# Attention values and output projections on two 64-row tiles of the matmul array, in two passes with the halves exchanged

## The chip, the cores and the metric

The kernel runs on one core of one Trainium2 chip. The metric is the time of one execution on the device in microseconds (us); the median of several runs is quoted. The profile's span is about 1.8 us shorter than the time of the same run. The execution of the kernel before that was profiled took 929.19 us, 1.0 above the median of its timed runs.

Engines are named as the profile names them: PE is the matrix engine (TensorE), PEld its weight loads, DVE VectorE, ACT ScalarE, POOL GpSimd.

## The reference

The input is one sequence of 2048 rows and 640 columns. After a layer norm, two branches follow; the change touches only the attention branch.

```python
q = (xn @ wq).reshape(B, Sq, 32, 192)              # 32 heads of 192
k, v = k_cache[:, :, -512:], v_cache[:, :, -512:]  # the last 512 keys
scores = einsum("bhqd,bhkd->bhqk", q, k) * 192 ** -0.5
o = einsum("bhqk,bhkd->bhqd", softmax(scores), v)
s = o.reshape(B, Sq, 32 * 192) @ wo                # 6144 -> 640
g = silu(mlp(xn))                                  # gated MLP, 640 -> 1536 -> 640
return x + s * g
```

## The kernel before

The attention works in units: four heads (a group g) and 512 query rows. There are 32 units. Units are taken two at a time; a pair is called a block here. A block first does all scores of its two units, interleaved with the query products of the next two (the stage S), then all values of its two units, interleaved with the output projections of the two units before (the stage V).

Queries and scores have contractions split into 64 rows, so they run on two row tiles of the array: `r = slice(i * H2, (i + 1) * H2)` with `H2 = 64`. The query product has a contraction of 128 rows, so it is done in two passes. In pass one, tile 0 makes the lower half's share of output 0 and tile 1 the upper half's share of output 1. In pass two they exchange outputs. Between the passes VectorE copies two columns of the result into `seen`, for no other purpose than to make pass two wait until pass one's writes have landed. Values and projections used the whole array:

```python
    def values(u, h, k):                       # one head: 512 rows x 192 (+1: the softmax sum)
        e = E[u, h // 2]
        o4 = wide(k).rearrange("p (q n) -> p q n", q=TQ)
        for q in range(TQ):                    # 4 x 4 matmuls of 128 rows x 193 columns
            for c in range(KC):
                nc.tensor.matmul(o4[:, q, 0:DH + 1], lhsT=e[:, c, h % 2, q * P:(q + 1) * P],
                                 rhs=vbuf[:, h, c, 0:DH + 1], start=(c == 0), stop=(c == KC - 1))
        ...
        nc.vector.reciprocal(rden[:], o4[:, :, DH:DH + 1])
        nc.vector.tensor_tensor(o_st[u][:, :, h * DH:(h + 1) * DH], o4[:, :, 0:DH],
                                rden[:].to_broadcast([P, TQ, DH]), ALU.mult)

    def project(u, q, k, out_eng):             # 128 rows: 6 x (512 + 128) columns
        for cc in range(GC):
            for d0, d1 in ((0, 512), (512, D)):
                nc.tensor.matmul(wide(k)[:, d0:d1], lhsT=oT[u][:, cc, q * P:(q + 1) * P],
                                 rhs=wo[:, cc, d0:d1], start=(cc == 0), stop=(cc == GC - 1))
        ...                                    # g == 0: copy; g > 0: acc = result + acc
                                               # last g: times the gate, plus acc, out

    order = (2, 3, 0, 1)
    for u0 in range(0, NU - 2, 2):             # one block
        for u in (u0, u0 + 1):                 # stage S
            for i, what in enumerate(((0, 0), (1, 0), (0, 1), (1, 1), (2, 0), None, (2, 1), None)):
                scores(u, *sc[i], i % 2)
                if what is not None:
                    queries(u + 2, what[0], 2 + (what[0] + u) % 2, what[1])
        ...
        for u in (u0, u0 + 1):                 # stage V
            for q in range(4):
                if u0 > 0:
                    values(u, q, order[2 * q % 4])
                    project(u - 2, q, order[(2 * q + 1) % 4], nc.sync)
                else:
                    values(u, q, order[q])
            turn_out(u)
```

The last argument of each function is the PSUM tile: there are four (0 to 3), each of two banks, and all matmuls of the kernel write to these four. Stage S uses 0 and 1 for scores and 2 and 3 for queries; stage V uses 2, 3, 0, 1 in turn.

The softmax here doesn't subtract the row's maximum and nothing guards it: scores larger than these inputs give would overflow.

## Time and profile before

The time is 928.18 us (927.81 to 928.33, 4 runs).

| what | reading |
|---|---|
| PE busy | 919.2 us of a span of 927.4 |
| PE share of the chain that ended last | 97% |
| granted clock | 0.999 |
| one block (S + V), from first score to first score | 47.23 us |
| PE waiting, in all | 3.2 us, all in start and tail |

The page's table of busy times (engine, us, share of the span, number of instructions), its two lines of the chain, and its four costliest matmul groups (line, operation, output and inputs, shape, count; then busy us and mean ns of one; then idle time before):

```profile
PE 919.2 (99%) x8004; PEld 547.2 (59%) x8004; DVE 467.2 (50%) x736; ACT 302.8 (33%) x333; POOL 126.0 (14%) x152
...
PE 97%; DMA 1%; DVE 1%; SPq 0%; issue 0%; ACT 0%; DVEq 0%; ACTq 0%
PE bank L457 21%; PE bank L421 21%; PE bank L437 18%; PE bank L403 18%; PE bank L250 10%; PE bank L262 6%; PE bank L369 1%; DMA wu_sb<-in_B_w_up_dram 1%; PE bank L300 1%; DVE gate L466 1%; DVE o_sb L461 1%; DMA oT<-o_st 1%; SPq L449 0%; PE bank L230 0%; ACT xnT L236 0%
...
L421 PE MATMUL bank<-xnT,wq_sb 64*128 64x512 bf16 x1800 | 223.7, 376 | 0.0
L457 PE MATMUL bank<-wo_sb,oT 128*128 128x512 bf16 x1344 | 200.8, 299 | 0.0
L403 PE MATMUL bank<-qT,kT 64*128 64x512 bf16 x1536 | 198.4, 376 | 0.0
L437 PE MATMUL bank<-vbuf,E 128*128 128x193 bf16 x2048 | 189.5, 247 | 0.0
```

L421 are the queries, L457 the projections (the mean of 299 ns mixes matmuls of 512 and of 128 columns), L403 the scores, L437 the values. The idle column is 0.0: by this page PE waits for nobody. The mean of one matmul (376 ns for a query) is not what a matmul costs in a stream, because matmuls overlap on record. What counts is the distance from one start to the next. It can be read from the timeline, where neighbours of one kind are merged (start, duration, engine and line, operation, count). Here is PE around a block end of the kernel before, and on DVE the evacuation (the copy out of PSUM) of the last values group; DVE's other instructions are left out:

```profile
257.01 1.50 PE L437 MATMUL bank<-vbuf,E 128*128 128x193 bf16 x16
258.35 1.79 PE L457 MATMUL bank<-wo_sb,oT 128*128 128x512 bf16 x12
258.76 0.96 DVE L443 TENSOR_TENSOR o_st<-bank,rden 128x768 bf16<-128x768 f32 x1
260.07 0.82 PE L403 MATMUL bank<-qT,kT 64*128 64x512 bf16 x6
260.73 1.24 PE L421 MATMUL bank<-xnT,wq_sb 64*128 64x512 bf16 x10
```

From 257.01 to 258.35, 16 values matmuls take 1.34 us: 83.4 ns each by the single records. From 260.73 the ten query matmuls, five pairs, take 1.08 us in the records: 216 ns per pair. From 258.35 to 260.07 a projection takes 1.72 us, but the same step between two values groups takes 1.63; the difference is the mode switch from 128 to 64 rows.

And the table of PE's waits, complete, says where PE stood still (us in total, times, longest):

```profile
PE bank L190 <- DVE eps_t L182: 1.2, 1, 1.2
PE bank L300 <- DMA wg_sb<-in_B_w_gate_dram: 1.0, 1, 1.0
PE bank L457 <- DMA oT<-o_st: 0.6, 1, 0.6
PE bank L300 <- DMA wu_sb<-in_B_w_up_dram: 0.4, 1, 0.4
```

### The profile page before, as it was taken

The page shows a single profiled execution, that of the slowest core. Times are in us where ns is not written, and L with a number is a line of the kernel's source. Part 1 is how long each engine was busy: PE and PEld are TensorE (multiplying, and loading weights), DVE is VectorE, ACT ScalarE, POOL GpSimd, SP SyncE. Part 2 cuts the span into 40 slices and gives each one's busy share as a digit, 9 for nine tenths or more (in the row PEclk, how much of TensorE's full clock was granted, in tenths as well). Part 3 has the DMA queues.
Part 4 walks back from the last instruction along what each step waited for, and adds up shares of the span by engine and source line. Part 5 has one row for each costly group of instructions (what it writes and reads, how often), then busy time and mean ns, then how long its engine had stood idle before and what let it go on. Part 6 is the DMA issues. An engine that isn't in the chain of part 4 may idle for free.

```text
span 927.4 us, 18043 instructions
## 1 busy us (share of the span) xinstructions
PE 919.2 (99%) x8004; PEld 547.2 (59%) x8004; DVE 467.2 (50%) x736; ACT 302.8 (33%) x333; POOL 126.0 (14%) x152
## 2 busy tenths in 40 slices
PE   8999999999999999999999999999999999999997
PEld 6445454465756565656565656566666656565665
DVE  5452522444645464545454555545554545454567
ACT  3222222255141424242423333332324242415240
POOL 1000110001002000200020011001100110175720
PEclk9999999999999999999999999999999999999999
DMA  9310340115424233333424152415251515253625
GB/s 318 80 22 8 88 86 1 43 60 87 82 58 111 78 69 70 97 92 41 97 87 103 39 99 78 111 35 104 65 111 40 110 61 98 66 115 96 102 74 125
DMA packets 162686, 76.68 MB, mean 83 GB/s; under 512 B 140944, under 2 KB 158176, under 8 KB 162608
## 3 DMA queue, kind: packets, MB, share of 16 engines
q1 hardware_dynamic: 155424, 53.64, 27.1%
q0 software_dynamic: 5808, 20.52, 7.9%
q8 instruction: 62, 1.02, 0.5%
q10 hardware_dynamic: 1376, 1.38, 0.4%
q14 instruction: 16, 0.13, 0.1%
HBM read 39.45 MB, written 2.62 MB: 45 GB/s over the span
## 4 chain that ended last, share of the span: by engine, by line
PE 97%; DMA 1%; DVE 1%; SPq 0%; issue 0%; ACT 0%; DVEq 0%; ACTq 0%
PE bank L457 21%; PE bank L421 21%; PE bank L437 18%; PE bank L403 18%; PE bank L250 10%; PE bank L262 6%; PE bank L369 1%; DMA wu_sb<-in_B_w_up_dram 1%; PE bank L300 1%; DVE gate L466 1%; DVE o_sb L461 1%; DMA oT<-o_st 1%; SPq L449 0%; PE bank L230 0%; ACT xnT L236 0%
## 5 line engine op out<-in xcount | busy, mean ns | idle before, releaser
L407 ACT ACTIVATE E<-bank 128x1024 bf16<-128x1024 f32 x256 | 255.8, 1024 | 456.8 <-PE bank L403 456.6
L421 PE MATMUL bank<-xnT,wq_sb 64*128 64x512 bf16 x1800 | 223.7, 376 | 0.0
L457 PE MATMUL bank<-wo_sb,oT 128*128 128x512 bf16 x1344 | 200.8, 299 | 0.0
L403 PE MATMUL bank<-qT,kT 64*128 64x512 bf16 x1536 | 198.4, 376 | 0.0
L437 PE MATMUL bank<-vbuf,E 128*128 128x193 bf16 x2048 | 189.5, 247 | 0.0
L437 PEld LDWEIGHTS <-E 128*128 128x128 bf16 x2048 | 168.6, 98 | 18.0 <-issue 6.4
L428 DVE CAST qT<-bank 128x1024 bf16<-128x1024 f32 x90 | 110.2, 1225 | 128.5 <-PE bank L421 128.5
L457 PEld LDWEIGHTS <-oT 128*128 128x128 bf16 x1536 | 121.0, 98 | 79.0 <-issue 1.3
L421 PEld LDWEIGHTS <-wq_sb 64*128 64x128 bf16 x1800 | 93.1, 100 | 102.2
L403 PEld LDWEIGHTS <-kT 64*128 64x128 bf16 x1536 | 74.0, 94 | 89.8 <-issue 4.8
L443 DVE TENSOR_TENSOR o_st<-bank,rden 128x768 bf16<-128x768 f32 x128 | 122.6, 958 | 4.4
L472 DVE TENSOR_TENSOR acc<-bank,acc 128x640 f32<-128x640 f32 x96 | 79.2, 825 | 43.3 <-PE bank L457 43.2
L118 POOL DMA_DIRECT2D vbuf<-in_A_v_cache_dram x28 | 21.1, 755 | 306.9 <-PE bank L437 304.0
L426 DVE COPY seen<-bank 128x2 f32<-128x2 f32 x90 | 14.4, 160 | 93.8 <-PE bank L421 93.8
L442 DVE RECIPROCAL rden<-bank 128x4 f32<-128x4 f32 x128 | 23.4, 183 | 65.1 <-PE bank L437 65.1
L250 PE MATMUL bank<-xnT,wu_sb 128*128 128x512 bf16 x220 | 54.7, 379 | 0.0
L250 PE MATMUL bank<-xnT,wg_sb 128*128 128x512 bf16 x220 | 54.7, 379 | 0.0
L262 PE MATMUL bank<-wd_sb,hT 128*128 128x512 bf16 (+1 forms) x384 | 52.8, 299 | 0.0
L256 DVE TENSOR_TENSOR hT<-bank,sig 128x512 bf16<-128x512 f32 x44 | 30.3, 690 | 43.7 <-ACT sig L253 43.7
L253 ACT ACTIVATE sig<-bank 128x512 bf16<-128x512 f32 x44 | 26.3, 597 | 68.4 <-PE bank L250 65.2
L262 PEld LDWEIGHTS <-hT 128*128 128x128 bf16 x384 | 29.7, 98 | 23.1
L250 PEld LDWEIGHTS <-wu_sb 128*128 128x128 bf16 x220 | 21.5, 98 | 26.0
(51 smaller groups left out, 317.7 us busy)
## 6 DMA issues: line engine op xcount, KB each, us to landing
wo_sb<-in_A_wo_dram SPq DMA_DIRECT2D x7, 960.0 KB, 5.3
wq_sb<-in_A_wq_dram POOLq DMA_DIRECT2D x7, 960.0 KB, 6.0
k_st<-in_A_k_cache_dram POOLq DMA_DIRECT2D x14, 384.0 KB, 5.2
vbuf<-in_A_v_cache_dram POOLq DMA_DIRECT2D x28, 192.0 KB, 3.3
row<-in_A_x_dram POOLq DMA_DIRECT2D x16, 160.0 KB, 2.8
oT<-o_st SPq DMA_TRANSPOSE x128, 2.6
x_sb<-in_A_x_dram SPq DMA_DIRECT2D x3, 640.0 KB, 9.4
wd_sb<-in_B_w_down_dram SPq DMA_DIRECT2D x1, 1920.0 KB, 12.9
```

Source lines behind the costliest of these rows:

```text
L250: nc.tensor.matmul(bank[k][:, half, 0:r1 - r0], lhsT=w[:, c, f * P:(f + 1) * P], rhs=xnT[:, b, c, r0:r1], start=(c == 0), stop=(c == NCD - 1))
L253: nc.scalar.activation(sig[:, 0:r1 - r0], bank[k][:, 0, 0:r1 - r0], AF.Sigmoid)
L256: nc.vector.tensor_tensor(hT[b][:, f, r0:r1], bank[k][:, 1, 0:r1 - r0], sig[:, 0:r1 - r0], ALU.mult)
L262: nc.tensor.matmul(wide(k)[:, d0:d1], lhsT=hT[b][:, f, q * P:(q + 1) * P], rhs=wd_sb[:, f, d0:d1], start=(f == 0), stop=(f == NF - 1))
L403: nc.tensor.matmul(bank[k][:, i, :], lhsT=kT[r, pr, j, c * P:(c + 1) * P], rhs=q[r, pr * DJ + j, :], start=(j == 0), stop=(j == DJ - 1))
L407: nc.scalar.activation(E[u, pr][:, c, :, :], bank[k][:], AF.Exp, scale=scale_qk)
L421: nc.tensor.matmul(bank[k][:, half, :], lhsT=wq[r, c, col:col + DJ * (P - 1) + 1:DJ], rhs=xnT[r, b, c, :], start=(c == 0 and not second), ...
L428: nc.vector.tensor_copy(qT[u][:, 2 * m:2 * m + 2, :], bank[k][:])
L437: nc.tensor.matmul(o4[:, q, 0:DH + 1], lhsT=e[:, c, h % 2, q * P:(q + 1) * P], rhs=vbuf[:, h, c, 0:DH + 1], start=(c == 0), stop=(c == KC ...
L443: nc.vector.tensor_tensor(o_st[u][:, :, h * DH:(h + 1) * DH], o4[:, :, 0:DH], rden[:].to_broadcast([P, TQ, DH]), ALU.mult)
L457: nc.tensor.matmul(wide(k)[:, d0:d1], lhsT=oT[u][:, cc, q * P:(q + 1) * P], rhs=wo[:, cc, d0:d1], start=(cc == 0), stop=(cc == GC - 1))
L472: nc.vector.tensor_tensor(acc[:, t, :], wide(k)[:, 0:D], acc[:, t, :], ALU.add)
```

## The change

The intent: let the whole attention run on two 64-row tiles, so that PE no longer switches between the modes. Values and projections are split as the queries were: two passes, halves exchanged, a tiny copy between the passes. To fill the time between the passes, two jobs are interleaved: values pass one, projection pass one, values pass two, projection pass two. The last eight projections stay on the full array.

```diff
     def values(u, h, k):
-        for q in range(TQ):
-            for c in range(KC):
-                nc.tensor.matmul(o4[:, q, 0:DH + 1], lhsT=e[:, c, h % 2, q * P:(q + 1) * P],
-                                 rhs=vbuf[:, h, c, 0:DH + 1], start=(c == 0), stop=(c == KC - 1))
+        for turn in range(2):
+            for qq in range(TQ // 2):
+                for c in range(KC):
+                    for i in range(2):
+                        r = slice(i * H2, (i + 1) * H2)
+                        q = (i ^ turn) * (TQ // 2) + qq
+                        nc.tensor.matmul(o4[:, q, 0:DH + 1],
+                                         lhsT=e[r, c, h % 2, q * P:(q + 1) * P],
+                                         rhs=vbuf[r, h, c, 0:DH + 1],
+                                         start=(turn == 0 and qq == 0 and c == 0),
+                                         stop=(turn == 1 and c == KC - 1), skip_group_check=True)
+            if turn == 0:
+                nc.vector.tensor_copy(seen[:, DJ, :], bank[k][:, :, 0])
+                yield
... (reciprocal and o_st as before)
-    def project(u, q, k, out_eng):
+    def project(u, q, k, out_eng, two=True):
+        res = bank[k][:, :, 0:HD]              # two halves of 320 columns, one per bank
+        for turn in range(2 if two else 1):
+            for cc in range(GC):
+                for i in range(2):
+                    r = slice(i * H2, (i + 1) * H2) if two else slice(0, P)
+                    half = i ^ turn
+                    nc.tensor.matmul(res[:, half, :], lhsT=oT[u][r, cc, q * P:(q + 1) * P],
+                                     rhs=wo[r, cc, half * HD:(half + 1) * HD], ...)
+            if two and turn == 0:
+                nc.vector.tensor_copy(seen[:, DJ + 1, :], bank[k][:, :, 0])
+                yield
... (what follows reads res in place of wide(k)[:, 0:D])
+    def together(*jobs):
+        for _ in range(2):
+            for j in jobs:
+                next(j, None)
...
-            for q in range(4):
-                if u0 > 0:
-                    values(u, q, order[2 * q % 4])
-                    project(u - 2, q, order[(2 * q + 1) % 4], nc.sync)
-                else:
-                    values(u, q, order[q])
+            if u0 > 0:
+                for q in range(4):
+                    together(values(u, q, order[2 * q % 4]),
+                             project(u - 2, q, order[(2 * q + 1) % 4], nc.sync))
+            else:
+                for q in (0, 2):
+                    together(values(u, q, order[q]), values(u, q + 1, order[q + 1]))
... (in the tail likewise: projections two at a time, values two at a time;
...  the last eight projections with two=False)
```

More of the change, by code (lines that the diff above doesn't have):

```diff
@@ L393 @@
     oT = {}
-    seen = acc_pool.tile([P, DJ, 2], F32, name="seen")
+    seen = acc_pool.tile([P, DJ + 2, 2], F32, name="seen")
     load_wo(0)
@@ L449, in turn_out @@
             nc.sync.dma_start_transpose(oT[u][:, :, q * P:(q + 1) * P], o_st[u][:, q, :])
-    def project(u, q, k, out_eng):
+    HD = D // 2
+    def project(u, q, k, out_eng, two=True):
         g, b = u // NB, u % NB
@@ L454, in project, with cols @@
         t = b * TQ + q
-        for cc in range(GC):
-            for d0, d1 in ((0, 512), (512, D)):
-                nc.tensor.matmul(wide(k)[:, d0:d1], lhsT=oT[u][:, cc, q * P:(q + 1) * P],
-                                 rhs=wo[:, cc, d0:d1], start=(cc == 0), stop=(cc == GC - 1))
+        def cols(x):
+            return x.rearrange("p (i n) -> p i n", i=2)
+        res = bank[k][:, :, 0:HD]
[5 more added lines that the diff above has]
+                    nc.tensor.matmul(res[:, half, :], lhsT=oT[u][r, cc, q * P:(q + 1) * P],
+                                     rhs=wo[r, cc, half * HD:(half + 1) * HD],
+                                     start=(turn == 0 and cc == 0),
+                                     stop=(cc == GC - 1 and (turn == 1 or not two)),
+                                     skip_group_check=two)
+            if two and turn == 0:
+                nc.vector.tensor_copy(seen[:, DJ + 1, :], bank[k][:, :, 0])
+                yield
         if g == NG - 1:
             o_sb = fin.tile([P, D], F32, name="o_sb", bufs=2)
-            nc.vector.tensor_tensor(o_sb[:], wide(k)[:, 0:D], gate[:, t, :], ALU.mult)
+            nc.vector.tensor_tensor(cols(o_sb[:]), res, cols(gate[:, t, :]), ALU.mult)
             r_sb = gate[:, t, :]
@@ L469, in project @@
         elif g == 0:
-            nc.vector.tensor_copy(acc[:, t, :], wide(k)[:, 0:D])
+            nc.vector.tensor_copy(cols(acc[:, t, :]), res)
         else:
-            nc.vector.tensor_tensor(acc[:, t, :], wide(k)[:, 0:D], acc[:, t, :], ALU.add)
+            nc.vector.tensor_tensor(cols(acc[:, t, :]), res, cols(acc[:, t, :]), ALU.add)
         if g == NG - 2:
@@ L477, in project @@
             nc.gpsimd.tensor_tensor(acc[:, t, :], acc[:, t, :], x_sb[:], ALU.add)
+        yield
+    def together(*jobs):
+        for _ in range(2):
+            for j in jobs:
+                next(j, None)
     sc = [(pr, c) for pr in range(2) for c in range(KC)]
@@ L516 @@
         scores(*sc[i], order[i % 4])
-    for q in range(2):
-        project(u - 2, q, q, nc.sync)
+    together(*(project(u - 2, q, q, nc.sync) for q in range(2)))
     for i in range(6, 12):
         scores(*sc[i], order[(i - 6) % 4])
-    for q in range(2, 4):
-        project(u - 2, q, q - 2, nc.sync)
+    together(*(project(u - 2, q, q - 2, nc.sync) for q in range(2, 4)))
     for i in range(12, 16):
         scores(*sc[i], order[i % 4])
-    for q in range(4):
-        project(u - 1, q, order[q], nc.sync)
+    for q in (0, 2):
+        together(*(project(u - 1, q + i, order[q + i], nc.sync) for i in range(2)))
     for v in (u, u + 1):
-        for h in range(4):
-            values(v, h, order[h])
+        for h in (0, 2):
+            together(*(values(v, h + i, order[h + i]) for i in range(2)))
         turn_out(v)
     for q in range(4):
-        project(u, q, order[q], nc.sync)
+        together(project(u, q, order[q], nc.sync, False))
     for q in range(4):
-        project(u + 1, q, order[q], nc.scalar if q < 3 else None)
+        together(project(u + 1, q, order[q], nc.scalar if q < 3 else None, False))
 _INS = ['A_x', 'A_k_cache', 'A_v_cache', 'A_wq', 'A_wo', 'B_x', 'B_w_gate', 'B_w_up', 'B_w_down']
```

## The prediction

> **What bounds the kernel.** TensorE: PE is busy 919 of 927 us (busy table), the chain of waits is 97% PE, and the granted clock is 1.0. The wait table shows PE waiting for nothing but 3 us of start and tail.
>
> **Issue times from the trace (start to start).** Values: 83.4 ns per full-array 128x193 matmul, 1.335 us per head. Projection: 216 + 56 ns per 512+128 columns, 1.63 us per tile. Queries and scores, already on two 64-row tiles: 216 ns per pair of 512 columns, the two members 3 to 7 ns apart. A pair costs what one full matmul costs, so splitting values and projections saves no streaming: 16 pairs of about 83 ns, and 12 of (320/512 of 213 + 2.7) = 136 ns, again 1.63 us.
>
> **What it saves.** Only mode switches. The Trainium skill ("TensorEngine Tiling (Array Packing)", Key Properties) says changing the tiling mode drains the TensorE; this trace agrees: the step from 64 to 128 rows takes 308 instead of 209 ns, the way back 151 instead of 56, so about 97 ns each. 29 of 31 switches go: -2.8 us.
>
> **What it adds.** 3488 matmuls (hidden, if issue keeps up) and about 250 tiny VectorE copies between the passes (160 ns, as those of the queries). The skill (same page, Gotcha 1) says row tiles may not access one PSUM bank simultaneously; hence pass two waits for that copy. VectorE works in order: the copies come behind the evacuations.
>
> Per values+projection step (2.97 us) VectorE needs 217 (reciprocal) + 875 (o_st) + 742 (acc) + 2x77 ns, about 2.0 us (spacings from the trace). Following order: the values copy ends about 1.38 us after the step's start and pass two wants to start at 1.48. It just fits.
>
> It does not fit in three places:
> 1. Block ends. The last values group now ends 0.82 us before the scores instead of 1.63, so its o_st (bank 0, which the first score needs) ends 0.6 us late: 14 blocks, about +8.5 us.
> 2. Values beside values (first block): the copy sits behind two o_st of 0.96 us, about 0.6 us per pair: +2 us.
> 3. Tail: projections beside projections with two 0.82 us multiplies or adds each, and values pairs: +6 us.
>
> A recurrence over both engines with these durations reproduces the kernel before (47.25 us per block against 47.23 in the trace) and gives about +14 us for the change. 60 ns more release latency or a slower 2x320 evacuation opens the wait in about 100 steps (+5 us). Values now need four PE instructions per 83 ns; the densest stretch of this trace does two per 56 ns. Each 10 ns more per pair would cost about 15 us.
>
> **Prediction:** 943 us, 80% range 935 to 964. Faster by over 2%: 0.01; within 2%: 0.62; slower by over 2%: 0.37.
>
> **What would show it.** Right: values pairs at 83 ns and projection pairs at 136; score matmuls waiting on o_st (0.5 to 0.7 us, once per block); PE waiting on the copies little in the steady steps, 0.6 us or more in first block and tail; the gaps of 308 and 151 ns gone; PE idle rising from 8 to over 20 us. Wrong: no wait at block ends, or values pairs at 95 ns or more.
>
> **What would make it wrong.** Issue rate (slower, over 950); pairs of short matmuls streaming better than full ones (faster); the copy's wait opening in every step.

## The result

The changed kernel takes 942.66 us (942.01 to 943.09, 4 runs) against 928.18 (927.81 to 928.33, 4 runs). The ratio is 1.0156, with a 95% interval of 1.0138 to 1.0174. Here and below, a ratio is the mean time of one kernel's fast runs over that of the other's fast runs of the same rounds, so it is not quite the ratio of the medians quoted.

The lines of the page after that answer to those of before:

```profile
PE 920.3 (98%) x11474; PEld 630.1 (67%) x11492; DVE 486.7 (52%) x984; ACT 302.7 (32%) x333; POOL 125.7 (13%) x152
...
PE 93%; DVE 5%; DMA 1%; issue 1%; DVEq 0%; ACT 0%; ACTq 0%
PE bank L421 21%; PE bank L482 20%; PE bank L403 18%; PE bank L443 17%; PE bank L250 10%; PE bank L262 5%; DVE o_st L456 3%; PE bank L369 1%; DVE o_sb L492 1%; DVE gate L497 1%; PE bank L300 1%; DMA wu_sb<-in_B_w_up_dram 1%; DVE rden L455 0%; PE bank L230 0%; DVE seen L450 0%
...
L482 PE MATMUL bank<-wo_sb,oT 64*128 64x320 bf16 x2688 | 222.8, 296 | 0.0
L443 PE MATMUL bank<-vbuf,E 64*128 64x193 bf16 x4096 | 212.6, 243 | 3.9 <-DVE seen L450 3.9
L403 PE MATMUL bank<-qT,kT 64*128 64x512 bf16 x1536 | 201.3, 376 | 6.7 <-DVE o_st L456 6.5
```

PE has 3,470 more matmuls on record and is busy only 1.1 us longer; that the tiles do not slow it down is shown by the starts below, since busy times rest on modelled ends. What is new is DVE's 5% in the chain, chiefly `o_st` (L456), and two idle figures that were 0.0. The waits of PE after, longest first; what is left out are waits of the start, as before, and two of 1.1 and 0.3 us in the tail:

```profile
PE bank L403 <- DVE o_st L456: 6.5, 14, 0.6
PE bank L443 <- DVE seen L450: 3.9, 7, 1.4
...
```

Fourteen waits of a score for `o_st`: one at the end of each of the 15 blocks but the last. A block now takes 47.82 us instead of 47.23. Timeline of PE and DVE at such a block end (weight loads, other engines and DVE's other instructions left out):

```profile
260.53 0.84 PE L443 MATMUL bank<-vbuf,E 64*128 64x193 bf16 x16
261.20 0.99 PE L482 MATMUL bank<-wo_sb,oT 64*128 64x320 bf16 x12
261.63 0.96 DVE L456 TENSOR_TENSOR o_st<-bank,rden 128x768 bf16<-128x768 f32 x1
262.64 0.82 PE L403 MATMUL bank<-qT,kT 64*128 64x512 bf16 x6 [0.45 <-DVE o_st L456]
```

The 16 half matmuls of a values pass, eight pairs, take 0.67 us from start to start (260.53 to 261.20), which is 83 ns per pair: exactly what a full matmul took before. The last values group ends where the projection's pass two begins, 0.82 us before the scores could start (261.20 + 12/2 x 0.136 = 262.01). Its evacuation `o_st` ends at 262.59 (261.63 + 0.96), so the first score, which writes the same PSUM tile 0, starts at 262.64 instead of 262.01: 0.63 us lost. Before, the whole projection of 1.63 us stood between the two, and the evacuation ended at 259.72, 0.35 us before the first score (260.07).

Note that the table says 0.45 us where 0.63 were lost. The profile counts idle time from the *end* of the last matmul, and the Trainium skill ("Perfetto Trace Analysis", Summary: the profiler window per engine type) calls the end on record for TensorE estimated. This trace shows what that does to a wait: a projection matmul is on record for 296 ns, while in a stream the next pair starts 116 ns after the second matmul of a pair (for values 243 and 64 ns). So about 0.18 us of such a wait are missing from the table, as here, and a shorter wait hardly appears. The following account is therefore made from starts: the distance of the first starts of neighbouring groups, less the normal spacing of what lies between (216, 83.4, 136 ns per pair; for full matmuls 215.8, 83.4 and 55.6 ns for 512, 193 and 128 columns). From the first score to the last matmul:

| us over the normal spacing | before | after |
|---|---|---|
| mode switches (36 and 2, about 97 ns each at the switch itself) | 3.5 | 0.2 |
| a DMA wait in the tail | 0.7 | 0 |
| first score of a block, waits for `o_st`: 13 x 0.63 + 0.78 | 0 | 9.0 |
| first projection of a block, 14 x 0.18 (see below) | 0 | 2.5 |
| copies behind evacuations, first block: 3 x 0.59 | 0 | 1.8 |
| the same and one score wait in the tail: 3 x 0.59 + 1.61 + 1.31 + 0.46 | 0 | 5.2 |
| sum of all differences | 4.3 | 18.0 |

(The last row is the sum over all groups; the rows above leave out many differences of a few ns, mostly negative, because the spacings taken as normal are rounded up.) The sums differ by 13.7 us; from the first score to the start of the last matmul the two executions differ by 757.9 - 743.8 = 14.1. (The spans differ by 941.1 - 927.4 = 13.7 too, but that is chance: the first score comes 0.5 us earlier in the changed kernel's execution, a difference of the parts that were not changed.) Hence the account is complete to about 0.4 us, which lies in the rounding of the spacings; there is no room in it for matmuls that are slower by more than that in sum.

The fourth row is a wait that was not looked for. The first projection of a block takes PSUM tile 3, which the last query of stage S used. Its result is copied out by VectorE from 285.52 to 286.74 us in one block; the projection starts at 286.80, 0.85 us after the values pass ahead of it, which itself needs 0.67. Before the change that values group lasted 1.34 us and covered the copy.

```profile
285.52 1.23 DVE L428 CAST qT<-bank 128x1024 bf16<-128x1024 f32 x1 [2.21 <-PE bank L421]
285.95 0.85 PE L443 MATMUL bank<-vbuf,E 64*128 64x193 bf16 x16
286.80 0.99 PE L482 MATMUL bank<-wo_sb,oT 64*128 64x320 bf16 x12
```

### The profile page after: what moved, and what is told of

Read it like the earlier page. It is cut to its first block, busy times and chain, and to the rows that moved or that the text cites. A ratio compares the mean times of both kernels' runs of the same rounds, so it can differ in the third digit from the quotient of the medians.

```text
span 941.1 us, 25256 instructions
## 1 busy us (share of the span) xinstructions
PE 920.3 (98%) x11474; PEld 630.1 (67%) x11492; DVE 486.7 (52%) x984; ACT 302.7 (32%) x333; POOL 125.7 (13%) x152
## 4 chain that ended last, share of the span: by engine, by line
PE 93%; DVE 5%; DMA 1%; issue 1%; DVEq 0%; ACT 0%; ACTq 0%
PE bank L421 21%; PE bank L482 20%; PE bank L403 18%; PE bank L443 17%; PE bank L250 10%; PE bank L262 5%; DVE o_st L456 3%; PE bank L369 1%; DVE o_sb L492 1%; DVE gate L497 1%; PE bank L300 1%; DMA wu_sb<-in_B_w_up_dram 1%; DVE rden L455 0%; PE bank L230 0%; DVE seen L450 0%
## 5 line engine op out<-in xcount | busy, mean ns | idle before, releaser
L421 PE MATMUL bank<-xnT,wq_sb 64*128 64x512 bf16 x1800 | 226.4, 376 | 0.0
L482 PE MATMUL bank<-wo_sb,oT 64*128 64x320 bf16 x2688 | 222.8, 296 | 0.0
L443 PE MATMUL bank<-vbuf,E 64*128 64x193 bf16 x4096 | 212.6, 243 | 3.9 <-DVE seen L450 3.9
L403 PE MATMUL bank<-qT,kT 64*128 64x512 bf16 x1536 | 201.3, 376 | 6.7 <-DVE o_st L456 6.5
L443 PEld LDWEIGHTS <-E 64*128 64x128 bf16 x4096 | 186.6, 94 | 15.6 <-issue 5.3
L482 PEld LDWEIGHTS <-oT 64*128 64x128 bf16 (+1 forms) x2976 | 166.2, 94 | 30.1 <-issue 3.9
L421 PEld LDWEIGHTS <-wq_sb 64*128 64x128 bf16 x1800 | 106.4, 100 | 88.9
L403 PEld LDWEIGHTS <-kT 64*128 64x128 bf16 x1536 | 86.4, 94 | 85.0 <-issue 10.5
L456 DVE TENSOR_TENSOR o_st<-bank,rden 128x768 bf16<-128x768 f32 x128 | 122.6, 958 | 4.4
L426 DVE COPY seen<-bank 128x2 f32<-128x2 f32 x90 | 14.4, 160 | 97.2 <-PE bank L421 97.2
L262 PE MATMUL bank<-wd_sb,hT 128*128 128x128 bf16 (+1 forms) x376 | 52.4, 297 | 0.4
L488 DVE COPY seen<-bank 128x2 f32<-128x2 f32 x120 | 19.1, 159 | 52.7 <-PE bank L482 51.4
```

Of the source, the lines that this page charges most:

```text
L262: nc.tensor.matmul(wide(k)[:, d0:d1], lhsT=hT[b][:, f, q * P:(q + 1) * P], rhs=wd_sb[:, f, d0:d1], start=(f == 0), stop=(f == NF - 1))
L403: nc.tensor.matmul(bank[k][:, i, :], lhsT=kT[r, pr, j, c * P:(c + 1) * P], rhs=q[r, pr * DJ + j, :], start=(j == 0), stop=(j == DJ - 1))
L421: nc.tensor.matmul(bank[k][:, half, :], lhsT=wq[r, c, col:col + DJ * (P - 1) + 1:DJ], rhs=xnT[r, b, c, :], start=(c == 0 and not second), ...
L443: nc.tensor.matmul(o4[:, q, 0:DH + 1], lhsT=e[r, c, h % 2, q * P:(q + 1) * P], rhs=vbuf[r, h, c, 0:DH + 1], start=(turn == 0 and qq == 0 a ...
L482: nc.tensor.matmul(res[:, half, :], lhsT=oT[u][r, cc, q * P:(q + 1) * P], rhs=wo[r, cc, half * HD:(half + 1) * HD], start=(turn == 0 and c ...
```

## The experiments

My theory: the tiles cost and save nothing in streaming; the change saves about 3 us of mode switches and loses it many times over to waits on VectorE, because results are finished later and the copies stand in VectorE's queue behind evacuations. Rivals: the 64-row matmuls with their doubled instructions are slower in themselves; or mode switches cost nothing real. All runs below gave correct results and were timed against the kernel before on the same chip.

### Other PSUM tiles for stage S (on the changed kernel)

The first score of a block takes tile 2, free for long, instead of tile 0; the queries take 3 and 1, so that the first projection of stage V (tile 3) does not meet a query whose result is still being copied out.

```diff
-                scores(u, *sc[i], i % 2)
+                scores(u, *sc[i], (2, 0)[i % 2])
-                    queries(u + 2, what[0], 2 + (what[0] + u) % 2, what[1])
+                    queries(u + 2, what[0], (3, 1)[(what[0] + u) % 2], what[1])
```

> The changed kernel with only the PSUM tiles of the scores (2 and 0 instead of 0 and 1) and of the queries (3 and 1 instead of 2 and 3) exchanged, so that the first group of a block after values and projections, and the first projection after the queries, find a tile that has long been read. Theory (waits): the 0.63 us wait before the first score of each block (8.2 us in 13 blocks, and 0.78 us once) and the 0.18 us before the first projection of each block (2.5 us in 14) go; nothing else moves. Expected 932 us, 930.5 to 934; one block from 47.82 to 47.1 us. Rival (the 64-row matmuls or their doubled instructions cost the time themselves, waits only hide it): 942 us, as before the exchange.

Measured: 931.11 us (929.81 to 931.97), ratio to the kernel before 1.0027 (1.0013 to 1.0040). The block takes 47.02 us. PE's waits, which are listed longest first, now begin with the copies; the line of `o_st`, 6.5 us, is gone:

```profile
PE bank L443 <- DVE seen L450: 3.9, 7, 1.4
...
```

By starts, the 13 x 0.63, the 0.78 and the 14 x 0.18 us are all gone: 11.5 us in sum, as much as the time fell (942.66 - 931.11). The edit moves scores and queries together; which of them is worth what (9.0 and 2.5) is read from the starts and was not run apart. The rival of slower tiles falls: the same matmuls, on the same tiles, are 11.5 us faster for the choice of a PSUM tile.

### The copies on ScalarE where they stood behind evacuations (on the changed kernel)

```diff
+    def look(j, k, act):
+        if act:
+            nc.scalar.activation(seen_a[:, j, :], bank[k][:, :, 0], AF.Copy)
+        else:
+            nc.vector.tensor_copy(seen[:, DJ + j, :], bank[k][:, :, 0])
...
-                    together(values(u, q, order[q]), values(u, q + 1, order[q + 1]))
+                    together(*(values(u, q + i, order[q + i], u + q > 0) for i in range(2)))
... (in the tail: act for the second pair of the last four tiled projections, and for all values)
```

> The changed kernel with the tiny copies between the passes done on ScalarE instead of VectorE, only in the first block (from its second pair on) and in the tail (values, and the second pair of the last four projections before them), where they sat behind evacuations. Theory (waits): the waits of 0.59 to 1.61 us there go, 6.5 us in all; blocks stay at 47.82 us. Expected 936.3 us, 934.5 to 938. Rival (what costs in the tail is the passes themselves): under 1 us gained.

Measured: 937.24 us (936.52 to 937.78), ratio 1.0091 (1.0076 to 1.0107): 5.4 us gained of the 6.5 expected. The waits for `seen` are gone from PE's table. Part of the gain came back as other waits in the tail: by starts, one score wait grew from 0.46 to 1.07 us, and a wait of 1.1 us for the DMA `oT` before the last projections appeared, where the changed kernel had lost time earlier. So the sum was right in kind and 1 us short in size.

### Both edits

> Both edits. Theory: the sum of both, since they remove different waits: 925.8 us, 924 to 928, that is 0.1 to 0.4% under the kernel before, because what is left of the change is its saving of mode switches (29 of 97 ns, 2.8 us). Rival (tiles themselves slower): over 930 us.

Measured: 926.05 us (924.37 to 927.17, 5 runs), the kernel before in the same rounds 928.42 (927.65 to 929.83, 9 runs), ratio 0.9971 (0.9958 to 0.9983). This version beats the kernel before, by 0.3%. What is left of PE's waits is in the start and the tail, nothing in the blocks:

```profile
PE bank L300 <- DMA wg_sb<-in_B_w_gate_dram: 1.3, 1, 1.3
PE bank L190 <- DVE eps_t L182: 1.2, 1, 1.2
PE bank L489 <- DMA oT<-o_st: 0.9, 1, 0.9
PE bank L300 <- DMA wu_sb<-in_B_w_up_dram: 0.4, 1, 0.4
PE bank L230 <- DVE xn L218: 0.2, 1, 0.2
```

A block takes 23.31 + 23.71 = 47.02 us, against 23.42 + 23.81 = 47.23 before: 0.1 us in each stage, one mode switch each. That is what the tiles are worth here. From the first score to the start of the last matmul it is 740.3 us against 743.8; the part before, loads and the gated MLP, differs between executions: the first score comes at 180.0 us in the profiled one of this version, at 178.6 in that of the kernel before, and at 177.2 to 178.6 in the others.

### Control: the other PSUM tiles in the kernel before

The same two lines as in the first experiment, in the kernel before.

> Control: the kernel before with the same exchange of PSUM tiles. It has no such wait (the last values group ends 1.63 us before the scores, its evacuation 0.25 us before), so theory: 928.2 us, within 0.5 us, blocks 47.23 us. Rival (the exchange is good by itself): several us faster, and then the gain of the first run says nothing of the change.

Measured: 928.66 us (928.38 to 928.82), ratio 1.0001 (0.9987 to 1.0015), blocks of 47.23 us. The exchange does nothing by itself; it only removes waits that the change made.

### More copies per step: how much room is there?

In the 112 steps of values with projections, the values' copy was done four times.

```diff
-                nc.vector.tensor_copy(seen[:, DJ, :], bank[k][:, :, 0])
+                for _ in range(4 if 0 < u < NU - 2 and u0 > 0 else 1):
+                    nc.vector.tensor_copy(seen[:, DJ, :], bank[k][:, :, 0])
```

> The changed kernel with the values' tiny copy done four times instead of once, in the 112 steps of values with projections alone. It tells how much room the copy has before pass two. Theory (it just fits, some 0.07 us to spare; each copy adds 77 ns on VectorE): three more copies are 231 ns, of which about 0.14 us per step come through: 958 us, 954 to 962. If VectorE has much room in the steps: 942.7, unchanged. If every copy were on the path already: 3 x 77 ns x 112 = 26 us, 968.

Measured: 995.44 us (994.16 to 995.96), ratio 1.0727 (1.0711 to 1.0743). That is 53 us over the changed kernel, twice what even the worst of the three expectations allowed. The experiment was flawed: all copies write the same column, so each waits for the one before. In VectorE's timeline, the four copies together take 0.74 us, single ones being on record for 0.16:

```profile
289.83 0.74 DVE L451 COPY seen<-bank 128x2 f32<-128x2 f32 x4
290.82 0.16 DVE L489 COPY seen<-bank 128x2 f32<-128x2 f32 x1 [0.25 <-PE bank L483]
```

By the records they start 193 ns apart, not 77. Three of them are 0.58 us per step; in the steady steps the trace shows 0.53 us lost, in 95 of them alike. The run thus agrees with little room (under 0.1 us), but its expectation had the wrong price of a copy. So it was repeated with a column for each copy.

```diff
-                for _ in range(4 if 0 < u < NU - 2 and u0 > 0 else 1):
-                    nc.vector.tensor_copy(seen[:, DJ, :], bank[k][:, :, 0])
+                for n in range(4 if 0 < u < NU - 2 and u0 > 0 else 1):
+                    nc.vector.tensor_copy(seen[:, DJ + (n and n + 1), :], bank[k][:, :, 0])
... (and three more columns in `seen`)
```

> The run with four copies again, but each copy writes columns of its own. In the run before all four wrote the same column, and the trace shows them 193 ns apart, each waiting for the one before, not 77 ns apart as the expectation assumed: 3 x 193 = 0.58 us per step, less some 0.1 us of room, times 112 is the 53 us that it cost. Theory (the copy has about 0.07 us of room in a step, independent copies follow each other after 77 ns): now 3 x 77 = 0.23 us, of which 0.14 to 0.16 us per step come through: 958 us, 954 to 962, and the copies 77 ns apart in the trace. If it stays near 995, the count of the copies costs that and not the chain of their writes.

Measured: 957.41 us (956.58 to 957.68), ratio 1.0315 (1.0298 to 1.0332). VectorE's timeline of a steady step and the copies of the next one, first of this run, then of the changed kernel:

```profile
292.73 0.96 DVE L457 TENSOR_TENSOR o_st<-bank,rden 128x768 bf16<-128x768 f32 x1
293.61 0.81 DVE L502 COPY acc<-bank 128x640 f32<-128x640 f32 x1
294.34 0.35 DVE L451 COPY seen<-bank 128x2 f32<-128x2 f32 x4
...
297.44 0.35 DVE L451 COPY seen<-bank 128x2 f32<-128x2 f32 x4
```

```profile
288.71 0.96 DVE L456 TENSOR_TENSOR o_st<-bank,rden 128x768 bf16<-128x768 f32 x1
289.58 0.81 DVE L501 COPY acc<-bank 128x640 f32<-128x640 f32 x1
290.31 0.15 DVE L450 COPY seen<-bank 128x2 f32<-128x2 f32 x1
...
293.28 0.15 DVE L450 COPY seen<-bank 128x2 f32<-128x2 f32 x1
```

Both show the order that the prediction followed: `o_st` and `acc` of the step before stand ahead of the copy, and the copy starts as soon as `acc` lets it (294.34 and 290.31; independent instructions overlap by some 80 ns on record). From copy to copy a step takes 3.10 us here and 2.97 in the changed kernel. The four independent copies start 67 ns apart (77 were expected) and take 0.35 us in all. By starts, PE loses 0.14 to 0.15 us in 95 steps: 3 x 67 = 0.20 us less 0.06 us of room. So in the changed kernel, "it just fits" is right to a few hundredths of a microsecond: any further work for VectorE in the steps comes out in the time. PE's table of waits shows hardly any of these 14 us (4.5 us for this copy against 3.9 before), since waits this short hide within the modelled ends; only the starts show them.

### Mode switches put back (on the version with both edits)

Projections within the 112 steps on the full array, whole, between the two passes of the values: two switches per step.

```diff
                     together(values(u, q, order[2 * q % 4]),
-                             project(u - 2, q, order[(2 * q + 1) % 4], nc.sync))
+                             project(u - 2, q, order[(2 * q + 1) % 4], nc.sync, False))
```

> The version with both edits, but the projections within the 112 steps again on the full array, between the two passes of the values, so that each step has two mode switches. Theory (a switch costs 97 ns of TensorE, a tiled pair costs what a full matmul costs): 224 x 0.097 = 21.7 us more than the version with both edits, 947.5 us, 945 to 950, the switch gaps in the trace again about 95 and 99 ns over the normal spacing. Rival (switches cost nothing when the queue is full; what differs is the tiles): within 3 us of the version with both edits.

Measured: 948.72 us (947.72 to 950.16), ratio 1.0230 (1.0213 to 1.0247): 22.7 us over the version with both edits (926.05), but on another chip, where the kernel before took 927.65. Each against the kernel before of its own rounds, it is (1.0230 - 0.9971) x 928 = 24.0 us. PE's timeline, first of this run, then of the version with both edits:

```profile
241.70 1.80 PE L489 MATMUL bank<-wo_sb,oT 128*128 128x320 bf16 x12
243.43 1.51 PE L450 MATMUL bank<-vbuf,E 64*128 64x193 bf16 x32
244.87 1.80 PE L489 MATMUL bank<-wo_sb,oT 128*128 128x320 bf16 x12
```

```profile
242.36 0.98 PE L489 MATMUL bank<-wo_sb,oT 64*128 64x320 bf16 x12
243.18 0.83 PE L450 MATMUL bank<-vbuf,E 64*128 64x193 bf16 x16
243.85 0.98 PE L489 MATMUL bank<-wo_sb,oT 64*128 64x320 bf16 x12
244.66 0.83 PE L450 MATMUL bank<-vbuf,E 64*128 64x193 bf16 x16
245.33 0.98 PE L489 MATMUL bank<-wo_sb,oT 64*128 64x320 bf16 x12
```

One step with switches takes 244.87 - 241.70 = 3.17 us, without 245.33 - 242.36 = 2.97. PE waited for nobody in either. By the records, the first full matmul starts 176 ns after the last half one (80 are normal), and the way back takes 232 ns (136 are normal): 96 ns at each switch, over two hundred of them alike. Another 11 ns are lost just behind it: the next full matmul comes after 147 ns instead of 136, the next pair of halves after 91 instead of 80. The expectation of 21.7 us had left these out. A switch thus costs 107 ns in all, and the 16 of a block are 1.71 us: a block takes 48.72 us here and 47.02 without them, and 14 such blocks differ by 23.9 us, which agrees with the 24.0 measured. The switches cost this although by the table PE waited for nobody, and this half-tiled version is slower than the kernel before and than the changed kernel (948.7 us against 928.2 and 942.7).

## Why the prediction was right

It said 943 us and 942.66 were measured, within its range and in its likeliest class. Point by point:

- *"A pair costs what one full matmul costs."* Right: 83 and 136 ns per pair. The fear that four instructions per 83 ns would not be sustained was unfounded; the eight pairs above take 0.67 us.
- *"Only mode switches ... -2.8 us."* Right in kind, with a miscount: the trace has 36 switches before and 2 after, not 31 and 2, so 34 went, and with the 11 ns behind each that makes 34 x 0.107 = 3.6 us. The Trainium skill ("TensorEngine Tiling (Array Packing)", Key Properties) has the drain, the traces have the size of the loss, 96 to 99 ns at the switch, and the run with switches put back pays it for 224 of them. Blocks are 0.21 us shorter with both edits, two switches each.
- *"Block ends ... +8.5 us."* Right: 9.0 us by starts, and the exchange of PSUM tiles removed it.
- *"Values beside values ... +2 us"*: 1.8. *"Tail ... +6 us"*: 5.2. ScalarE's copies removed the part of it that lay in the copies.
- *"It just fits."* Right, with 0.06 us to spare by the repeated copies run.

Four things were off and nearly cancelled. The text named three places where it doesn't fit; there was a fourth, the 14 waits of 0.18 us (2.5 us) of a block's first projection. Against it stand the tail term, 0.8 us too large; the saving, 0.8 us too small; and 0.7 us of a wait for a DMA in the tail of the kernel before, which the changed kernel, later there, no longer met. The hit to a microsecond is therefore partly luck; the terms are right to about 1 us each, but for the one left out. "PE idle rising from 8 to over 20 us" was also right in kind (8 to 941.1 - 920.3 = 21), but that figure is only as good as the modelled ends of matmuls.

One thing stays open. A direct check that the copies are needed (that two tiles may not write one PSUM bank at once) was not made, since taking the wait away alone would be a race.

## What to carry to other kernels

Cutting a product into passes with a hand-over between them moves the end of every result later and puts a new entry in another engine's queue: before trying it, follow that engine's queue in order, step by step, and look above all at the seams (block ends, the first and last iterations), where the filler between the passes is missing. A whole-array and a row-tiled stream cost the same per column here, so the only gain was in mode switches: in a case like this, count them and multiply by 0.1 us before rewriting anything. Where a matrix engine that is always busy gains small waits, measure from start to start: its waits by recorded ends are too small, and short ones vanish.

## What the Trainium skill lacked or had wrong

- "TensorEngine Tiling (Array Packing)", Key Properties, says that a change of mode drains the engine, but not what it costs: 96 to 99 ns at the switch in either direction, and 11 ns more just behind it, in the kernel before and in the run with switches put back.
- The same page, When to Use Tiling, gives row tiling only for contractions up to 64. No page has the case of a contraction of 128 split over two 64-row tiles: a pair takes what one full matmul takes (216 ns at 512 columns; 83 ns at 193), so nothing is gained but the mode switch.
- No page gives a sustained rate for a stream of weight loads and short matmuls on two row tiles: four instructions (two loads, two matmuls) per 83 ns were sustained, without loss against 83.4 ns per full pair of load and matmul.
- "TensorE: Matmul & The Clock Gate", Back-to-back issue gap, gives a sustained 131 ns per matmul of 512 columns for streams of load and matmul. Here it is 216 ns in every such stream, which fits the formula for isolated gaps on the same page.
- "Perfetto Trace Analysis", Identifying the Most-Contended Engine, recommends the busy share of weight loads, beside MFU (the share of the peak matmul rate that is used), as a measure of distance to the limit. Here it rose from 59% to 67% while the kernel became 1.6% slower, because each product has two loads instead of one.
- "Perfetto Trace Analysis" calls the end of a matmul estimated, but not what follows for waits: 0.18 us of each wait at a block end is missing from the profile here (0.45 shown where 0.63 were lost), and 14 us of waits of 0.14 us each hardly show at all.
- No page says how much farther apart small VectorE copies come when each overwrites the result of the one before: 193 ns from start to start, against 67 ns when they are independent.
